# Moving work between banks and engines in a fused attention and expert kernel: two attention banks, four for the first product, a relu half on POOL

## The chip, the cores and the metric

The kernel runs on one core of a Trainium2 chip. A core has five engines that run side by side, each through its own instructions in order: PE (TensorE) multiplies matrices and writes to PSUM; DVE (VectorE) and ACT (ScalarE) work element by element on PSUM and SBUF; POOL (GpSimd) does so on SBUF alone; SP (SyncE) here only issues DMA transfers. They wait for each other by semaphores. PSUM has eight banks of 128 partitions by 2 KiB, so one bank holds 128 x 512 float32. The metric is the device time of one execution in microseconds (us). Three runs of the kernel before gave 575.06, 575.25 and 577.19 us, a median of 575.25. The profile is of one further execution, whose own time is 574.72 us.

## The reference: what is computed

Two blocks, one after the other, all in float32.

```python
def phi(x):                       # x: (4, 4, 1088, 32); S1, S2: (8, 32)
    a = np.einsum('rd,bhsd->bhsr', S1, x)
    b = np.einsum('rd,bhsd->bhsr', S2, x)
    return np.einsum('bhsi,bhsj->bhsij', a, b).reshape(*x.shape[:-1], 64)
q_p, k_p = phi(q), phi(k)
kv = np.einsum('bhsf,bhsd->bhfd', k_p, v)
z = np.sum(k_p, axis=2)
num = np.einsum('bhsf,bhfd->bhsd', q_p, kv)
den = np.einsum('bhsf,bhf->bhs', q_p, z)[..., None] + 1e-06
x = (num / den).transpose(0, 2, 1, 3).reshape(4352, 128)

p = domain_probs / (domain_probs.sum(-1, keepdims=True) + 1e-09)   # (4352, 4)
for e in range(4):                # w1: (4, 128, 1024), w2: (4, 1024, 128)
    out += p[:, e:e + 1] * (np.maximum(x @ w1[e], 0.0) @ w2[e])
```

The attention is linear: the keys of a batch are first summed into `kv`, then queries of any number can be answered. The second block is a two-layer network for each of four experts, whose outputs are added up with weights from `domain_probs`.

## The kernel before

**Chunks, steps, halves.** The 4352 tokens are columns, in chunks of 128, 448, 512, 512, 512, 512, 512, 512, 320, 256 and 128 (`CHUNKS`). A chunk has 16 steps (`kq` from 0 to 15): four experts by four pairs of blocks, and a block is 128 of an expert's 1024 hidden units. A step has two halves, j = 0 and 1, one block each. `first(i, work)` makes the first product of step i, `second(i)` the second product; the main loop calls `first(i)` and then `second(i - 2)` (`LA` is 2), so the second product runs two steps behind. The first and last chunk (`plain`) use float32 matmuls; what follows is of the nine between.

**Split numbers.** A float32 matmul is made of three matmuls on split operands. The tokens of a chunk are split by `token_parts` into xa, xb, xd, the first weights by `weight_parts` into wa, wb, wd, half of the second weights by `second_weight_parts` into `vab` (two parts in one tile) and `vd`. Each split is an ACT scaling followed by two subtractions; on DVE these are scalar_tensor_tensor operations through the helper `stt` (line 685), which scale and subtract at once; the last token part is a subtraction on POOL. Of the split weights, 24 pieces are made in all, one a step from step 5 on (`to_part`); the token pieces of a chunk are made in step 12 of the chunk before, those of the first split chunk in the last step of the plain one.

**One half of `first`** (lines 868 to 888). PE: xa by wa and xb by wb into bank `g1` (lines 871, 872), xd by wd into bank `g2` (873). ACT: `t` = scaled `g1` (875). DVE: `t` = `t` - `g2` (877). For j = 0 the relu of `t` is split again, as input of the second product: ACT makes `hb` and `ha` (894, 895), DVE corrects `hb` (898, reading `t` and `hb`), POOL subtracts `hd` = `ha` - `hb` (901). For j = 1 the relu is plain: ACT makes `hid` from `t` (887). These later operations are put into lists and emitted by `flush` one half later: `hb` and `ha` after the `t` of half j = 1; DVE's `hb` and POOL's `hd` after the subtraction of half j = 1; `hid` after the `t` of the next step's half j = 0. `work()` at the end of a half emits pieces of the attention, as many as a running account of due columns asks for.

**`second`** adds four matmuls into the two output banks: `ha`, `hb`, `hd` by their weights (950 to 952) and `hid` by plain float32 weights (954, issued as two passes). When an expert's four steps are done, that is, in every fourth call of the loop (steps 1, 5, 9 and 13 of a chunk), `gather` brings the sums out: ACT copies `ev` and `ew` (978, 979), and POOL adds them (980), multiplies by the gate (984 for the first expert, else 986) and adds to `total` (987).

**Buffers.** PSUM has three banks `h` for `g1` and `g2` in turn, two for the outputs (`o0`, `o1`), one `f` and two `den`, `num` for the attention. In SBUF the pool `mpool` has two buffers for each name unless told otherwise. `t` is told nothing, so its halves alternate: the `t` of j = 0 always has one buffer and that of j = 1 the other; `ha`, `hb`, `hd` and `hid` have three, `ev`, `ew` and `ob` one. A write waits until the readers of the buffer's former contents are through; the framework puts that wait in by itself. Each engine's order is the order in which the code emits (`manual_schedule`).

**Attention.** `front` yields the attention's pieces: `keys(b)` turns, projects (in three banks `f`, `den`, `num`), multiplies and sums the keys of a batch; `queries(b, c, n)` projects queries in `f`, works on them on DVE, and `attend` multiplies them by the summed keys in `den` and `num`, divides and stores them to memory, from where they come back as columns.

Of the kernel before, what the change touches and what calls it, by code (L numbers as in the profile page):

```python
# [8 lines left out]
F32 = mybir.dt.float32  # L9
# [15 lines left out]
def kernel(  # L25
# [51 lines left out]
    mpool = ctx.enter_context(tc.tile_pool(name="moe", bufs=2))  # L77
    ps_h = ctx.enter_context(tc.tile_pool(name="ps_h", bufs=3, space=bass.MemoryType.PSUM))
    ps_o = ctx.enter_context(tc.tile_pool(name="ps_o", bufs=1, space=bass.MemoryType.PSUM))
    ps_f = ctx.enter_context(tc.tile_pool(name="ps_f", bufs=1, space=bass.MemoryType.PSUM))  # L80
    ps_n = ctx.enter_context(tc.tile_pool(name="ps_n", bufs=1, space=bass.MemoryType.PSUM))
    dram = ctx.enter_context(tc.tile_pool(name="dram", bufs=1, space=bass.MemoryType.DRAM))
# [52 lines left out]
    def load_w2(e, j, to=None):  # L135
        w2_of[e, j] = cpool.tile([P, FB // 2, DM], F32, tag=f"w2_{e}{j}", name="w2_sb")[:, :, :] if to is None else to
        nc.sync.dma_start(w2_of[e, j], w2[e].rearrange("(f j p) d -> j p f d", j=2, p=P)[j])

# [309 lines left out]
    def keys(b):  # L448
        for r in range(3):
            key_turn(b, r)  # L450
            yield
        kf = []
        for gi, (pool, tag) in enumerate(((ps_f, "f"), (ps_n, "den"), (ps_n, "num"))):
            kf.append(psum(pool, tag))
            key_project_wide(b, gi, kf[gi])
            if gi:
                key_add(b, gi - 1, kf[gi - 1])
            yield
        for _ in value_copy(b):
# [10 lines left out]
        kv = psum(ps_f, "f")  # L470
        for p in range(2):
            key_sum(b, p, kv)
            yield
        key_blocks(b, kv)
        yield
# [48 lines left out]
    def attend_first(b, c, n, qp):  # L524

        nd = [psum(ps_n, "den"), psum(ps_n, "num")]
        for _ in range(2):
# [31 lines left out]
    def attend(b, c, n, qp):  # L559
# [3 lines left out]

        nd = [psum(ps_n, "den"), psum(ps_n, "num")]
        W = H * (D + 1)
# [74 lines left out]
    def queries(b, c, n):  # L640
        qc = early.pop((b, c), None)
        if qc is None:
            qT = query_turn(b, c, n)
            yield
            yield
            yield
            qc = psum(ps_f, "f")
            nc.tensor.matmul(qc[:, 0:n], sq[:, :], qT[:, 0:n], start=True, stop=True)
            yield
# [33 lines left out]

    def stt(out, in0, scalar, in1, op1):
        nc.vector.scalar_tensor_tensor(out=out, in0=in0, scalar=scalar, in1=in1, op0=ALU.mult, op1=op1)  # L685

    def weight_parts(e):

        HF = F // 2
        for c in (slice(0, HF), slice(HF, F)):  # L690
            nc.scalar.activation(wa[:, e, c], w1_of[e][:, c], ACTF.Copy, scale=4096.0 * NEAR)
            stt(wb[:, e, c], w1_of[e][:, c], 4096.0, wa[:, e, c].bitcast(F32), ALU.subtract)
            yield
            stt(wd[:, e, c], wa[:, e, c].bitcast(F32), R12, wb[:, e, c].bitcast(F32), ALU.subtract)
            yield
# [5 lines left out]
    def second_weight_parts(e):  # L701

        w = w2_of[e, 0]
        vab = cpool.tile([P, 2, FB // 2, DM], F32R, tag=f"w1_{e}", name="vab")
        va, vb = vab[:, 0], vab[:, 1]
        nc.scalar.activation(va, w, ACTF.Copy, scale=4096.0 * NEAR)
        stt(vb, w, 4096.0, va.bitcast(F32), ALU.subtract)
        yield
        vd = cpool.tile([P, FB // 2, DM], F32R, tag=f"w2_{e}0", name="vd")
        stt(vd[:, :, :], va.bitcast(F32), -R12, vb.bitcast(F32), ALU.add)  # L710
        w2_parts[e] = va, vb, vd
        yield
# [3 lines left out]
    def load_last():  # L716

        for e, (tag, width) in enumerate((("kn", S), ("vn", H * NT * D), ("qn", S), ("qn", S))):
            w1_of[e] = lpool.tile([P, width], F32, tag=tag, bufs=2 if tag == "qn" else 1, name="w1_last")
            nc.sync.dma_start(w1_of[e][:, 0:F], w1[e])  # L720
            if e == 0:
                w_last[0] = apool.tile([P, E, FB // 2, DM], F32, tag="kp", name="w2_last")
            load_w2(e, 0, w_last[0][:, e])
# [3 lines left out]
    def token_parts(m):  # L727
# [4 lines left out]
        nc.scalar.activation(xa[:, 0:n], x, ACTF.Copy, scale=R12 * NEAR)  # L732
        stt(xb[:, 0:n], xa[:, 0:n].bitcast(F32), -4096.0, x, ALU.add)
        nc.gpsimd.tensor_tensor(
            out=xd_[:, 0:n], in0=xa[:, 0:n].bitcast(F32), in1=xb[:, 0:n].bitcast(F32), op=ALU.subtract
        )
        xparts[m] = xa, xb, xd_

    def start():
# [16 lines left out]
        for _ in value:  # L756
            pass
        fq = [psum(ps_o, "o0"), psum(ps_o, "o1"), psum(ps_n, "num")]
        for i in range(3):
# [12 lines left out]
        key_product(b, 4, 4, 1, 1, nc.vector, kf[1])  # L772
        kv = psum(ps_f, "f")
        for t0, n0 in ((0, 4), (4, 5)):
# [58 lines left out]

    def first(i, work):

# [32 lines left out]
        for j in range(2):  # L868
# [15 lines left out]
            else:  # L884
                u = hidden()[:, 0:n]
                hid[i].append(u)
                later[ACT].append(lambda t=t, u=u: nc.scalar.activation(u, t, ACTF.Relu))  # L887
# [22 lines left out]

    def second(i):
        m, kq = steps[i]
        n, (e, f) = CHUNKS[m], divmod(kq, NP)
        hd = hid.pop(i)
        if plain(m):
# [3 lines left out]
            for j in range(2):  # L919
                for _ in range(2):  # L920
                    on_side(
                        lambda s: acc[m][half[s], 0:DM],
                        lambda s: hd[j][:, HP * s : HP * s + HP],
                        lambda s: w2_of[e, j][:, f, :],
                        start=(f == j == 0),
# [16 lines left out]
            return  # L942
        if f == 0:
# [3 lines left out]
        for j in range(2):  # L947
            if j < FK:
                (va, vb, vd), (ha, hb, hc) = w2_parts[e], hd[j]
                nc.tensor.matmul(o0, va[:, f, :], ha, start=(f == j == 0), stop=False)  # L950
                nc.tensor.matmul(o0, vb[:, f, :], hb, start=False, stop=(last and j == FK - 1))  # L951
                nc.tensor.matmul(o1, vd[:, f, :], hc, start=(f == j == 0), stop=False)  # L952
            else:
                nc.tensor.matmul(o1, w2_of[e, j][:, f, :], hd[j], start=False, stop=(last and j == 1))  # L954

# [68 lines left out]
    for i in range(len(steps) + LA):  # L1024
        if i < len(steps):
# [17 lines left out]

            first(i, work)
            if i > NQ - 12:
# [58 lines left out]
```

## Time and profile before

| | before |
|---|---|
| median of three runs | 575.25 us |
| profiled execution: its time, its span | 574.72 us, 572.9 us |
| PE busy | 501.9 us (88%) |
| DVE busy | 432.4 us (75%) |
| ACT busy | 424.5 us (74%) |
| POOL busy | 318.6 us (56%) |
| start and first plain chunk, until the first `xd,wd` matmul | 35.1 us |
| chunk of 448, to the same matmul of the next chunk | 69.3 us |
| chunks of 512 | 61.4, 62.6, 61.7, 64.3, 61.4, 61.3 us |
| chunks of 320 and of 256 | 41.9 and 34.5 us |
| last plain chunk, output | 19.4 us |

How to read the rows. The page gives for each engine the time in which it is busy, its share of the span and the instructions. The busy time of PE is modelled, since matmuls are pipelined. A row of a group of instructions has line, engine, operation, the tile written and the tiles read (buffer numbers left out), the shape, the count, then busy time, mean duration in ns, idle time of the engine just before them, and what ended that idle time. A row of the waits reads: engine and line that waited, the engine and line waited for, total us, times, longest. A row of a stretch has its bounds and length, then the busy time and count of PE, PEld (weight loads), DVE, ACT and POOL, the granted PE clock, the share of the DMA engines and GB/s. A row of the order of events has start, duration, engine, line, operation, tiles, and in brackets idle time before it.

### The profile page before, as it was taken

Reading aid. Unit: us, or ns where it says so; the run is one execution under the profiler, and the core shown is the slowest. Engines: PE = TensorE matmul, PEld = TensorE weight load, DVE = VectorE, ACT = ScalarE, POOL = GpSimd, SP = SyncE. Lnnn points to the kernel's source line nnn. Section 1 sums busy time; section 2 is a strip of 40 time slices with the busy share of each in tenths; the row PEclk is TensorE's granted clock in tenths of the full one; section 3 lists DMA queues with packets and bytes.
Section 4 is the critical chain, followed back from the end, with each engine's and each line's share of the span. In section 5 each row is a group of like instructions: output and inputs, shape, how many; then the busy total and the mean of one; then the engine's idle time right before and its main releaser. Section 6 shows DMA issues by size and latency. Waiting matters only on the chain.

```text
span 572.9 us, 9123 instructions
## 1 busy us (share of the span) xinstructions
PE 501.9 (88%) x2893; PEld 337.0 (59%) x2893; DVE 432.4 (75%) x792; ACT 424.5 (74%) x877; POOL 318.6 (56%) x298
## 2 busy tenths in 40 slices
PE   8967977989889998999798999899899888888887
PEld 5944554646555565555464556555455555666677
DVE  6969979597978777888878776778867886666643
ACT  3566766778778886878778785788778777887861
POOL 5142455456666567556565465656665666566550
PEclk9989998999999999999999998999999999999999
DMA  7661020511111212312022100021003000300700
GB/s 228 195 147 42 20 56 2 136 35 37 39 25 36 43 32 68 88 23 61 5 55 38 23 24 19 19 38 48 12 12 67 7 5 13 67 10 19 221 13 15
DMA packets 45480, 29.25 MB, mean 51 GB/s; under 512 B 26264, under 2 KB 40952, under 8 KB 45432
## 3 DMA queue, kind: packets, MB, share of 16 engines
q1 hardware_dynamic: 45416, 28.68, 19.5%
q8 instruction: 22, 0.36, 0.3%
q14 instruction: 26, 0.21, 0.1%
q10 hardware_dynamic: 16, 0.00, 0.0%
HBM read 24.42 MB, written 4.24 MB: 50 GB/s over the span
## 4 chain that ended last, share of the span: by engine, by line
PE 40%; DVE 27%; ACT 23%; issue 7%; DMA 1%; ACTq 0%; POOL 0%; SPq 0%; DVEq 0%
ACT t L875 13%; DVE t L877 9%; PE o L954 9%; DVE hb L898 9%; PE h L873 8%; PE h L871 4%; PE h L872 4%; ACT hid L887 3%; PE o L950 3%; PE o L951 3%; DVE qp L517 3%; PE o L952 3%; ACT hb L894 3%; ACT ha L895 2%; PE h L208 2%
## 5 line engine op out<-in xcount | busy, mean ns | idle before, releaser
L901 POOL TENSOR_TENSOR hd<-ha,hb 128x512 fp32r<-128x512 f32 (+3 forms) x144 | 173.2, 1203 | 206.5 <-PE h L872 74.9
L877 DVE TENSOR_TENSOR t<-t,h 128x512 f32<-128x512 f32 (+3 forms) x288 | 179.8, 625 | 116.6 <-ACT t L875 89.5
L875 ACT ACTIVATE t<-h 128x512 f32<-128x512 f32 (+3 forms) x288 | 158.9, 552 | 100.9 <-DVE hb L898 47.3
L871 PE MATMUL h<-xa,wa 128*128 128x512 f32 (+3 forms) x288 | 162.7, 565 | 12.6 <-DVE t L877 11.2
L873 PE MATMUL h<-xd,wd 128*128 128x512 f32 (+3 forms) x288 | 121.2, 421 | 48.6 <-ACT t L875 45.3
L954 PE MATMUL o<-hid,w_sb 128*128 128x512 f32 (+3 forms) x288 | 135.7, 553 | 0.0
L873 PEld LDWEIGHTS h<-xd,wd 128*128 128x128 f32 x288 | 54.4, 189 | 103.8 <-ACT t L875 96.9
L898 DVE SCALAR_TENSOR_TENSOR hb<-t,hb 128x512 fp32r<-128x512 f32 (+3 forms) x144 | 113.8, 790 | 0.3 <-ACT hb L894 0.3
L872 PE MATMUL h<-xb,wb 128*128 128x512 f32 (+3 forms) x288 | 106.8, 371 | 0.7 <-DVE xb L685 0.7
L894 ACT ACTIVATE hb<-t 128x512 fp32r<-128x512 f32 (+3 forms) x144 | 83.0, 576 | 16.0 <-DVE t L877 14.3
L871 PEld LDWEIGHTS h<-xa,wa 128*128 128x128 f32 x288 | 55.1, 191 | 58.4 <-DVE t L877 26.6
L887 ACT ACTIVATE hid<-t 128x512 f32<-128x512 f32 (+3 forms) x144 | 83.4, 579 | 0.0
L895 ACT ACTIVATE ha<-t 128x512 fp32r<-128x512 f32 (+3 forms) x144 | 82.5, 573 | 0.0
L872 PEld LDWEIGHTS h<-xb,wb 128*128 128x128 f32 x288 | 55.2, 192 | 31.1 <-issue 25.5
L954 PEld LDWEIGHTS o<-hid,w_sb 128*128 128x128 f32 x288 | 53.3, 191 | 9.2
L952 PE MATMUL o<-hd,vd 128*128 128x512 f32 (+3 forms) x144 | 54.1, 376 | 3.1 <-DVE vd L685 2.5
L950 PE MATMUL o<-ha,vab 128*128 128x512 f32 (+3 forms) x144 | 55.0, 382 | 0.0
L951 PE MATMUL o<-hb,vab 128*128 128x512 f32 (+3 forms) x144 | 53.7, 373 | 0.0
L980 POOL TENSOR_TENSOR ev<-ev,ew 128x512 f32<-128x512 f32 (+3 forms) x36 | 43.1, 1196 | 2.5 <-ACT ew L979 2.5
L987 POOL TENSOR_TENSOR total<-total,ev 128x512 f32<-128x512 f32 (+3 forms) x27 | 36.4, 1348 | 2.1
L986 POOL TENSOR_TENSOR ev<-ev,gate 128x512 f32<-128x512 f32 (+3 forms) x27 | 34.8, 1290 | 2.1
L952 PEld LDWEIGHTS o<-hd,vd 128*128 128x128 f32 x144 | 27.4, 190 | 8.4 <-POOL ev L986 2.8
(149 smaller groups left out, 495.7 us busy)
## 6 DMA issues: line engine op xcount, KB each, us to landing
gate<-gates SPq DMA_DIRECT2D x16, 256.0 KB
kn<-in_k_dram SPq DMA_DIRECT2D x4, 544.0 KB
vn<-in_v_dram SPq DMA_DIRECT2D x16, 128.0 KB
w_sb<-in_moe_w_dram SPq DMA_DIRECT2D x4, 512.0 KB
w_sb<-in_moe_w_dram SPq DMA_DIRECT2D x8, 256.0 KB
w_last<-in_moe_w_dram SPq DMA_DIRECT2D x4, 512.0 KB
gate<-gates SPq DMA_DIRECT2D x8, 224.0 KB
qn<-in_q_dram SPq DMA_DIRECT2D x2, 544.0 KB
```

The lines of the kernel that those rows point to most:

```text
L871: nc.tensor.matmul(g1[:, 0:n], wa[:, e, c], xa, start=True, stop=False)
L872: nc.tensor.matmul(g1[:, 0:n], wb[:, e, c], xb, start=False, stop=True)
L873: nc.tensor.matmul(g2[:, 0:n], wd[:, e, c], xd_, start=True, stop=True)
L875: nc.scalar.activation(t, g1[:, 0:n], ACTF.Copy, scale=1.0 + R12)
L877: nc.vector.tensor_tensor(out=t, in0=t, in1=g2[:, 0:n], op=ALU.subtract)
L887: later[ACT].append(lambda t=t, u=u: nc.scalar.activation(u, t, ACTF.Relu))
L894: nc.scalar.activation(hb, t, ACTF.Relu, scale=NEAR)
L895: nc.scalar.activation(ha, t, ACTF.Relu, scale=NEAR * R12)
L898: nc.vector.scalar_tensor_tensor(out=hb, in0=t, scalar=0.0, in1=hb.bitcast(F32), op0=ALU.max, op1=ALU.subtract)
L901: nc.gpsimd.tensor_tensor(out=hc, in0=ha.bitcast(F32), in1=hb.bitcast(F32), op=ALU.subtract)
L952: nc.tensor.matmul(o1, vd[:, f, :], hc, start=(f == j == 0), stop=False)
L954: nc.tensor.matmul(o1, w2_of[e, j][:, f, :], hd[j], start=False, stop=(last and j == 1))
```

## The change

- PSUM: the attention has two banks, `n` and `f`, in one pool instead of three; the banks `h` are four instead of three. In `keys` the three projections take `f`, `n`, `f`, and the addition that reads a bank is emitted ahead of the next projection.
- Order on PE: where the second product of step i - 2 is not the first of its expert, its half j = 0 (three matmuls) is emitted between the two halves of the first product of step i, and its half j = 1 after them.
- The pieces of weights and tokens: each DVE operation that scales and subtracts becomes an ACT scaling into a temporary tile (`tw`, in the buffers of `ob`, `ev` or `ew`) and a subtraction on POOL.
- The plain relu of `t` for j = 1 goes to POOL in odd steps, through `rectify`.
- The tiles of the second weights are two-dimensional instead of three-dimensional, with the same contents.

The diff, cut to these:

```diff
-    ps_h = ctx.enter_context(tc.tile_pool(name="ps_h", bufs=3, space=bass.MemoryType.PSUM))
+    ps_h = ctx.enter_context(tc.tile_pool(name="ps_h", bufs=4, space=bass.MemoryType.PSUM))
...
-    ps_f = ctx.enter_context(tc.tile_pool(name="ps_f", bufs=1, space=bass.MemoryType.PSUM))
-    ps_n = ctx.enter_context(tc.tile_pool(name="ps_n", bufs=1, space=bass.MemoryType.PSUM))
+    ps_a = ctx.enter_context(tc.tile_pool(name="ps_a", bufs=1, space=bass.MemoryType.PSUM))
...
-        for gi, (pool, tag) in enumerate(((ps_f, "f"), (ps_n, "den"), (ps_n, "num"))):
-            kf.append(psum(pool, tag))
-            key_project_wide(b, gi, kf[gi])
+        for gi, tag in enumerate(("f", "n", "f")):
             if gi:
                 key_add(b, gi - 1, kf[gi - 1])
+            kf.append(psum(ps_a, tag))
+            key_project_wide(b, gi, kf[gi])
             yield
...
-        nd = [psum(ps_n, "den"), psum(ps_n, "num")]
+        nd = [psum(ps_a, "n"), psum(ps_a, "f")]
...
-    def stt(out, in0, scalar, in1, op1):
-        nc.vector.scalar_tensor_tensor(out=out, in0=in0, scalar=scalar, in1=in1, op0=ALU.mult, op1=op1)
+    def scaled(tag, w, scale, dtype=F32):
+
+        t = mpool.tile([P, CW], F32, tag=tag, bufs=1, name="tw")[:, :]
+        nc.scalar.activation(t[:, 0 : w.shape[-1]].bitcast(dtype), w, ACTF.Copy, scale=scale)
+        return t
+
+    def minus(out, in0, in1):
+        nc.gpsimd.tensor_tensor(out=out, in0=in0, in1=in1, op=ALU.subtract)
...
         for c in (slice(0, HF), slice(HF, F)):
-            nc.scalar.activation(wa[:, e, c], w1_of[e][:, c], ACTF.Copy, scale=4096.0 * NEAR)
-            stt(wb[:, e, c], w1_of[e][:, c], 4096.0, wa[:, e, c].bitcast(F32), ALU.subtract)
-            yield
-            stt(wd[:, e, c], wa[:, e, c].bitcast(F32), R12, wb[:, e, c].bitcast(F32), ALU.subtract)
+            w, a, b, d = (x[:, c] for x in (w1_of[e], wa[:, e], wb[:, e], wd[:, e]))
+            nc.scalar.activation(a, w, ACTF.Copy, scale=4096.0 * NEAR)
+            minus(b, scaled("ob", w, 4096.0), a.bitcast(F32))
+            yield
+            minus(d, scaled("ev", w, NEAR, F32R), b.bitcast(F32))
             yield
...
-        stt(xb[:, 0:n], xa[:, 0:n].bitcast(F32), -4096.0, x, ALU.add)
-        nc.gpsimd.tensor_tensor(
-            out=xd_[:, 0:n], in0=xa[:, 0:n].bitcast(F32), in1=xb[:, 0:n].bitcast(F32), op=ALU.subtract
-        )
+        minus(xb[:, 0:n], x, scaled("ew", x, NEAR, F32R)[:, 0:n])
+        minus(xd_[:, 0:n], xa[:, 0:n].bitcast(F32), xb[:, 0:n].bitcast(F32))
...
-                later[ACT].append(lambda t=t, u=u: nc.scalar.activation(u, t, ACTF.Relu))
+                later[ACT].append(lambda t=t, u=u: rectify(u, t, kq % 2))
             work()
+            if between and j == 0:
+                between(0)
+
+    def rectify(u, t, on_pool):
+        if on_pool:
+            nc.gpsimd.tensor_scalar(out=u, in0=t, scalar1=0.0, scalar2=None, op0=ALU.max)
+        else:
+            nc.scalar.activation(u, t, ACTF.Relu)
...
-            first(i, work)
+            parted = i >= LA and not plain(steps[i - LA][0]) and not plain(m) and steps[i - LA][1] % NP
+            first(i, work, (lambda j: second(i - LA, j)) if parted else None)
...
-            second(i - LA)
+            second(i - LA, 1 if i < len(steps) and parted else None)
```

More of the change, by code (lines that the diff above doesn't have):

```diff
@@ L135, in load_w2 @@
     def load_w2(e, j, to=None):
-        w2_of[e, j] = cpool.tile([P, FB // 2, DM], F32, tag=f"w2_{e}{j}", name="w2_sb")[:, :, :] if to is None else to
-        nc.sync.dma_start(w2_of[e, j], w2[e].rearrange("(f j p) d -> j p f d", j=2, p=P)[j])
+        w2_of[e, j] = cpool.tile([P, FB // 2 * DM], F32, tag=f"w2_{e}{j}", name="w2_sb")[:, :] if to is None else to
+        nc.sync.dma_start(
+            w2_of[e, j].rearrange("p (f d) -> p f d", d=DM), w2[e].rearrange("(f j p) d -> j p f d", j=2, p=P)[j]
+        )
     load_rows(k, 0, "kn")
@@ L469, in keys @@
         yield
-        kv = psum(ps_f, "f")
+        kv = psum(ps_a, "n")
         for p in range(2):
@@ L524, in attend_first @@
     def attend_first(b, c, n, qp):
-        nd = [psum(ps_n, "den"), psum(ps_n, "num")]
+        nd = [psum(ps_a, "n"), psum(ps_h, "h")]
         for _ in range(2):
@@ L559, in attend @@
     def attend(b, c, n, qp):
-        nd = [psum(ps_n, "den"), psum(ps_n, "num")]
+        nd = [psum(ps_a, "n"), psum(ps_a, "f")]
         W = H * (D + 1)
@@ L646, in queries @@
             yield
-            qc = psum(ps_f, "f")
+            qc = psum(ps_a, "f")
             nc.tensor.matmul(qc[:, 0:n], sq[:, :], qT[:, 0:n], start=True, stop=True)
@@ L703, in second_weight_parts @@
         w = w2_of[e, 0]
[L704 to L707, printed above, removed]
+        vab = cpool.tile([P, 2, FB // 2 * DM], F32R, tag=f"w1_{e}", name="vab")
+        a, b = vab[:, 0], vab[:, 1]
+        nc.scalar.activation(a, w, ACTF.Copy, scale=4096.0 * NEAR)
+        minus(b, scaled("ob", w, 4096.0), a.bitcast(F32))
         yield
-        vd = cpool.tile([P, FB // 2, DM], F32R, tag=f"w2_{e}0", name="vd")
-        stt(vd[:, :, :], va.bitcast(F32), -R12, vb.bitcast(F32), ALU.add)
-        w2_parts[e] = va, vb, vd
+        u = scaled("ev", w, NEAR, F32R)
+        d = cpool.tile([P, FB // 2 * DM], F32R, tag=f"w2_{e}0", name="vd")[:, :]
+        minus(d, b.bitcast(F32), u)
+        w2_parts[e] = a, b, d
         yield
@@ L721, in load_last @@
             if e == 0:
-                w_last[0] = apool.tile([P, E, FB // 2, DM], F32, tag="kp", name="w2_last")
+                w_last[0] = apool.tile([P, E, FB // 2 * DM], F32, tag="kp", name="w2_last")
             load_w2(e, 0, w_last[0][:, e])
@@ L757, in start @@
             pass
-        fq = [psum(ps_o, "o0"), psum(ps_o, "o1"), psum(ps_n, "num")]
+        fq = [psum(ps_o, "o0"), psum(ps_o, "o1"), psum(ps_a, "n")]
         for i in range(3):
@@ L772, in start @@
         key_product(b, 4, 4, 1, 1, nc.vector, kf[1])
-        kv = psum(ps_f, "f")
+        kv = psum(ps_a, "f")
         for t0, n0 in ((0, 4), (4, 5)):
@@ L832, in half_columns, with first @@
             )
-    def first(i, work):
+    def first(i, work, between=None):
         m, kq = steps[i]
@@ L909, in flush, with second @@
                 later[w].pop(0)()
-    def second(i):
+    def second(i, j=None):
         m, kq = steps[i]
         n, (e, f) = CHUNKS[m], divmod(kq, NP)
-        hd = hid.pop(i)
+        hd = hid[i] if j == 0 else hid.pop(i)
         if plain(m):
@@ L923, in second @@
                         lambda s: hd[j][:, HP * s : HP * s + HP],
-                        lambda s: w2_of[e, j][:, f, :],
+                        lambda s: w2_of[e, j][:, DM * f : DM * (f + 1)],
                         start=(f == j == 0),
@@ L942, in second @@
             return
-        if f == 0:
+        if f == 0 and j in (0, None):
             acc[m, e] = psum(ps_o, "o0"), psum(ps_o, "o1")
@@ L946, in second @@
         last = f == NP - 1
-        for j in range(2):
+        w = slice(DM * f, DM * (f + 1))
+        for j in range(2) if j is None else (j,):
             if j < FK:
                 (va, vb, vd), (ha, hb, hc) = w2_parts[e], hd[j]
-                nc.tensor.matmul(o0, va[:, f, :], ha, start=(f == j == 0), stop=False)
-                nc.tensor.matmul(o0, vb[:, f, :], hb, start=False, stop=(last and j == FK - 1))
-                nc.tensor.matmul(o1, vd[:, f, :], hc, start=(f == j == 0), stop=False)
+                nc.tensor.matmul(o0, va[:, w], ha, start=(f == j == 0), stop=False)
+                nc.tensor.matmul(o0, vb[:, w], hb, start=False, stop=(last and j == FK - 1))
+                nc.tensor.matmul(o1, vd[:, w], hc, start=(f == j == 0), stop=False)
             else:
-                nc.tensor.matmul(o1, w2_of[e, j][:, f, :], hd[j], start=False, stop=(last and j == 1))
+                nc.tensor.matmul(o1, w2_of[e, j][:, w], hd[j], start=False, stop=(last and j == 1))
     def turn_back(m, src):
@@ L1061 @@
         if i == LA:
-            made_hp[3] = psum(ps_n, "num")
+            made_hp[3] = psum(ps_h, "h")
             for c in (0, HP):
```

## The prediction

> **What bounds the kernel now.** I read the page's sums first, then the stretches of the trace chunk by chunk, then the waits, then the order of events in one undisturbed stretch. On the page:
>
> ```profile
> span 572.9 us, 9123 instructions
> PE 501.9 (88%) x2893; PEld 337.0 (59%) x2893; DVE 432.4 (75%) x792; ACT 424.5 (74%) x877; POOL 318.6 (56%) x298
> ```
>
> No engine is full. The stretches (PE, PEld, DVE, ACT, POOL busy) are cut at the first `xd,wd` matmul of a chunk; here are one chunk of 512 columns, the one of 320 and the one of 256:
>
> ```profile
> 354.40:415.80 61.40, 54.99 (x242) 34.23 (x240) 49.02 (x83) 48.35 (x89) 36.40 (x28) 1.00 0.13 28
> 477.10:519.00 41.90, 35.13 (x179) 27.45 (x178) 27.18 (x55) 34.24 (x89) 25.49 (x28) 1.00 0.13 30
> 519.00:553.50 34.50, 28.41 (x176) 23.83 (x174) 20.88 (x49) 28.57 (x89) 20.18 (x27) 1.00 0.33 101
> ```
>
> The six chunks of 512 take 61.4, 62.6, 61.7, 64.3, 61.4 and 61.3 us, 372.7 together, so four steps take 15.5 us and one step 3.9. The 448 chunk takes 69.3 (35.1 to 104.4), the start 35.1, the last plain chunk 19.4. What is waited for (us in total, times, longest):
>
> ```profile
> PEld h L873 <- ACT t L875: 96.9, 133, 2.0
> DVE t L877 <- ACT t L875: 89.5, 152, 2.4
> ACT t L875 <- DVE hb L898: 47.3, 52, 2.1
> PE h L873 <- ACT t L875: 45.3, 83, 1.6
> ```
>
> Lines 1 and 4 are the three banks: the third matmul of a half takes the bank that the ACT evacuation of the half before has to free. Line 3 is another ring: `t` has two buffers, so the `t` of a half j=0 waits until the DVE operation of line 898, one step earlier, has read its buffer. Keep that ring in mind. The order of events, undisturbed:
>
> ```profile
> 417.98 0.60 ACT L875 ACTIVATE t<-h 128x512 f32<-128x512 f32 x1
> 418.47 0.62 ACT L894 ACTIVATE hb<-t 128x512 fp32r<-128x512 f32 x1
> 418.61 0.69 DVE L877 TENSOR_TENSOR t<-t,h 128x512 f32<-128x512 f32 x1 [0.46 <-ACT t L875]
> 418.99 0.62 ACT L895 ACTIVATE ha<-t 128x512 fp32r<-128x512 f32 x1
> 419.21 0.68 DVE L898 SCALAR_TENSOR_TENSOR hb<-t,hb 128x512 fp32r<-128x512 f32 x1
> 420.07 1.28 POOL L901 TENSOR_TENSOR hd<-ha,hb 128x512 fp32r<-128x512 f32 x1 [1.90 <-PE h L872]
> 420.57 0.62 ACT L887 ACTIVATE hid<-t 128x512 f32<-128x512 f32 x1
> ```
>
> The durations come from here; the steps between engines too: 0.04 us from ACT to DVE and back, 0.18 from DVE (419.89) to POOL (420.07). POOL to PE is 0.06 elsewhere (`xd` ends 35.02, its matmul starts 35.08).
>
> **The change, part by part.**
>
> *Four banks, alternating products.* They remove the bank wait: in the chain a bare step is 3.25 us (0.50 third matmul + 1.55 second product + 0.47 + 0.61 ACT and 0.12 between), while the matmuls alone take 9 x 0.23 + 0.86 = 2.93. The gain is at most 0.32 a bare step and more in disturbed ones, if nothing else is late. What is late next decides, so I count no gain here; it is in the walk below and in rival 1.
>
> *Attention in two banks.* Its pieces run one after another, and the addition is now emitted ahead of the projection that takes its bank. Cover: the pieces between. Without it, three batches wait about 1 us each; bounds 0 to 3, taken 0.
>
> *Half of the plain relu on POOL.* This is the step that counts. Odd steps give ACT 0.62 us less. But `t` keeps two buffers: the `t` of half j=1 in step i+1 (ACT) overwrites what POOL's relu of step i reads, and so now waits for it. On POOL that relu is emitted behind `hd` of step i, and in every second odd step also behind the three gather operations (ev, product, total). Queued behind the waiting `t` on ACT are `hb`, `ha` and the next `t`; waiting for those are DVE, the bank of the next first product, and through `hb` the very `hd` that the next POOL relu is queued behind. That closes a loop over two steps, counted from the start of such a `t` (512 columns, i odd):
>
> - ACT t 0 to 0.60; DVE subtraction 0.64 to 1.33, hb 1.33 to 2.02 (ACT's hb and ha end at 1.84);
> - ACT t j=0 of step i+2 needs that hb: 2.06 to 2.66, ACT relu to 3.28, t j=1 to 3.88;
> - DVE subtraction 3.92 to 4.61, hb to 5.30; POOL hd 5.48 to 6.76;
> - POOL relu 6.83 to 6.83 + r; 0.06 later the next `t` that waits for POOL starts.
>
> So a pair of steps takes 6.89 + r, and every second pair has the gather in it: 3 x (1.285 + 0.07) = 4.06 us, by the medians of lines 980, 986 and 984 (987 has 1.425, partly beside DVE). Its ACT copies (1.2) hide under hd. PE hides as well: its next matmuls are released at 0.64 and 2.70 and need 2.9 a step.
>
> The relu on POOL is not in the trace. Nearest rows:
>
> ```profile
> L734 POOL TENSOR_TENSOR xd<-xa,xb 128x512 fp32r<-128x512 f32 x6 | 7.7, 1282 | 4.4 <-DVE xb L685 4.4
> L782 POOL COPY sq<-s_T 32x32 f32<-32x32 f32 x4 | 0.8, 203 | 0.2
> L174 POOL MEMSET sr<- 128x768 f32 x1 | 0.7, 742 | 0.0
> L263 POOL COPY sr<-sp 32x192 f32<-32x192 f32 x2 | 0.7, 338 | 0.1
> L282 POOL TENSOR_SCALAR dsum<-dsum 128x34 f32<-128x34 f32 x1 | 0.2, 224 | 0.1
> L173 POOL MEMSET sk<- 128x128 f32 x1 | 0.2, 205 | 0.3 <-POOLq L1088 0.3
> ```
>
> The two copies give 0.84 ns an element above 0.18: 0.61 at 512. The same operation at 34 elements gives 1.41 ns: 0.90. I take the middle, r = 0.75 (448: 0.68, 320: 0.54, 256: 0.46). Bounds: the memsets, 0.53, and two inputs, 1.28. The Trainium skill's "GPSIMD Engine Reference", Elementwise, has 769 ns for a tight loop over 512 elements; as an estimate that would make r = 0.77 and the sum 1 us longer.
>
> Four steps of 512: 2 x 7.64 + 4.06 = 19.34, a chunk 77.4. On top, per chunk: 1.0 for the second ACT operation of the token pieces; 0.6 for half of ACT's attention copies (2.7 a batch, half a batch a chunk); 2.0 for DVE attention pieces of 0.7 us where the loop leaves only 0.5 to 0.7 (eight pairs by 0.25): 81.0, against 62.1. Six chunks: 485.7 - 372.7 = **+113**.
> The 320 chunk by its rows (t 0.44, relu 0.465, subtraction 0.49, hd 0.88): pair 5.06 + 0.54, gather 2.83: 8 x 5.60 + 4 x 2.83 + 2 = 58.1: **+16.2**. The 256 chunk: pair 4.88, gather 2.4: 8 x 4.88 + 9.6 + 0.5 = 49.1: **+14.6**.
>
> *Pieces of weights and tokens.* 32 subtractions leave DVE (0.99 mean for wb, 1.475 for xb) for POOL (1.28), with 32 more ACT operations (0.62). In the 448 chunk 13 of the 24 weight pieces fall into the loop: the six in odd steps sit on POOL between hd and relu (6 x 1.35 = 8.1); in even steps ACT gets 0.4 beyond its slack (six: 2.4). Chunk: 8 x 6.88 + 3 x 3.6 + 8.1 + 2.4 + 2 = 78.3 against 69.3: **+9**. In the first 35 us, 11 pieces of 1.35 go through POOL from about 20 us, with 3.2 us of ring copies, then two token operations of 1.2: ready at about 40.4 instead of 35.1: **+5** (bounds 0, if POOL starts with the first weights, and 8).
>
> Sum: 113 + 16.2 + 14.6 + 9 + 5 = 158 on the profiled execution's 574.7: **732 us**. That execution lies 0.5 below the median of 575.25, which changes nothing at this size. The last plain chunk keeps its 19.4.
>
> Ends: with r = 0.53, no extras and no loss at the start: 6 x 75.6 - 372.7 = 81, 12 + 12 for the short chunks, 3 for 448: 683. With r = 1.28, 72 waits of 0.5 more: 768; with all the extras doubled (six by 3.6) 790.
>
> A rule that speaks against the change: line 898 takes 0.684 median, but 0.866 mean at 512, up to 1.79, where POOL works beside it. The Trainium skill's "SBUF — State Buffer", Who interferes with whom, says that a DVE instruction with two SBUF inputs and a GpSimd one that reads SBUF exclude each other for whole instructions. By it, busier POOL would add 0.58 to each colliding hb; if half of 144 collide, 42 us. By the walk the two run in turn (POOL idle from 0 to 2.0 and 4.6 to 5.5), so I add nothing.
>
> **Rivals.**
> 1. *Faster: the wait on POOL does not decide.* Then four steps take what the fullest engine needs: PE 11.7 + 1.4 of attention = 13.1, ACT 12.2 + 0.8, DVE about 12, POOL 11.3. Halfway between 13.1 and 15.5, at 14.2, 24 groups of four win 31, the short chunks 4, and 5 are lost at the start: 545. For it: the bank waits (142 us on PE) really go. Against: it needs two pairs and the gather to stay under 15.5 together; even with the gather outside, two pairs are 15.3. It decides only if POOL's relu starts before hd and the gather.
> 2. *Same: the gather hides, the relu wait stays.* 15.3 for 15.5, extras against bank waits: 575.
> 3. *POOL's relu costs as much as two inputs:* 768.
> 4. *The clock falls.* PE would stand about 4 us in every gather pair; at half clock for a while, 1 us more in each of 35 groups: 767. The page has the clock under full in 3 of 40 slices, without such gaps.
>
> **How the numbers follow.** The forecast has 0.65, rival 3 0.12, rival 4 0.10, a milder loop (under 690) 0.06, rival 1 0.04, rival 2 0.03. Rivals 3 and 4 end near 770, the bounds at 683 and 790: the range is 680 to 790, outside of which lie rivals 1 and 2 and parts of the others, about 0.15. Slower has 0.93, same 0.03, faster 0.04; half a per cent, 2.9 us, is about what a measurement of this kernel can tell.
>
> **What would show it.** In the profile after: ACT's `t` waiting for POOL's `hid` as the largest wait, over 150 us in some 72 waits, long (over 4 us) in every second; four steps of 512 at 19 to 20 us; POOL's relu at 0.6 to 0.9; the old waits of the third matmul for ACT `t` mostly gone, replaced by PE waiting for `t` behind POOL; ACT and PE shares down to about 60 to 70%. A `t` that hardly waits for POOL, or relus on POOL ahead of the gather, would make all this wrong. Weight pieces: the 448 chunk near 78 us, its start near 40.

## The result and the profile after

The changed kernel takes 762.61 us (median of four runs, 762.04 to 763.53), the kernel before 576.13 (four runs, 575.06 to 577.19). The ratio is 1.324, with a 95% interval of 1.320 to 1.327: 186 us slower. The prediction said 732 us in a range of 680 to 790. The direction and the place were right; the sum is 30 us short.

The profiled execution took 762.66 us, with these rows on its page: the sums by engine, the granted clock in 40 slices, the shares of the chain that ended last, POOL's relu and DVE's `hb` (line 913 is line 898 of before).

```profile
span 760.9 us, 9052 instructions
PE 582.0 (76%) x2893; PEld 375.0 (49%) x2893; DVE 384.7 (51%) x759; ACT 404.7 (53%) x838; POOL 445.4 (59%) x403
...
PEclk9888887999998888999988989988988999889899
...
POOL 33%; PE 29%; ACT 13%; DVE 12%; issue 9%; DMA 2%; SPq 1%; POOLq 0%; ACTq 0%; DVEq 0%
...
L901 POOL TENSOR_SCALAR hid<-t 128x512 f32<-128x512 f32 (+3 forms) x72 | 99.7, 1385 | 0.0
...
L913 DVE SCALAR_TENSOR_TENSOR hb<-t,hb 128x512 fp32r<-128x512 f32 (+3 forms) x144 | 92.7, 644 | 0.0
```

No engine is full, as before, but POOL, which was nowhere on the chain of before (0%), now makes the largest share of it with only 59% of its time busy. The chain of before, for comparison:

```profile
PE 40%; DVE 27%; ACT 23%; issue 7%; DMA 1%; ACTq 0%; POOL 0%; SPq 0%; DVEq 0%
```

A share of busy time does not show a bound of this kind; the waits of the changed kernel do:

```profile
DVE t L884 <- ACT t L882: 332.3, 223, 6.4
ACT t L882 <- POOL hid L901: 249.3, 65, 6.5
PEld h L878 <- ACT t L882: 186.9, 137, 5.4
...
PE h L878 <- ACT t L882: 124.2, 56, 4.9
PEld h L880 <- DVE t L884: 51.5, 118, 2.4
...
PE f L393 <- DVE fs L403: 12.7, 2, 6.7
...
PEld o L969 <- POOL vd L692: 8.9, 1, 8.9
PE o L969 <- POOL vd L692: 8.6, 1, 8.6
```

The second row is the new one: ACT stands 249 us before 65 of its `t`, until POOL's relu has read the buffer. DVE and PE then stand behind ACT (first, third and fourth row). Line 878 is the first matmul of a half; the old waits of the third matmul (now 880) for ACT's `t` have shrunk from 142 us to 7.6. So the four banks did what they were for, but only in part: the third matmul now waits 65 us for DVE's `t` (51.5 of them in the fifth row), against 0.7 before, and PE stands longest one matmul further on, at the first of the next half.

The stretches, cut as those of before: the chunk of 448, one of 512, those of 320 and 256 (length; then busy time of PE, PEld, DVE, ACT, POOL; granted clock; DMA share and GB/s):

```profile
39.10:128.70 89.60, 63.27 (x268) 41.09 (x269) 46.58 (x82) 49.61 (x105) 56.91 (x47) 0.83 0.21 47
128.70:211.20 82.50, 65.84 (x274) 37.54 (x272) 44.80 (x83) 43.07 (x80) 48.32 (x36) 0.92 0.10 26
634.70:691.80 57.10, 44.09 (x178) 32.04 (x176) 23.56 (x53) 30.40 (x80) 34.54 (x37) 0.88 0.10 22
691.80:740.20 48.40, 38.19 (x175) 28.67 (x174) 19.16 (x49) 26.24 (x80) 26.50 (x35) 0.89 0.24 72
```

| stretch, us | before | predicted | after |
|---|---|---|---|
| start | 35.1 | 40.4 | 39.1 |
| chunk of 448 | 69.3 | 78.3 | 89.6 |
| six of 512 | 372.7 | 485.7 | 506.0 |
| chunk of 320 | 41.9 | 58.1 | 57.1 |
| chunk of 256 | 34.5 | 49.1 | 48.4 |
| last plain chunk | 19.4 | 19.4 | 20.7 |

The loop itself, in the timeline of an undisturbed pair of steps (165.13 to 173.17) and a pair with the gather in it (173.17 to 185.15). Some rows are left out; a bracket gives the idle time before and what ended it:

```profile
165.13 0.60 ACT L882 ACTIVATE t<-h 128x512 f32<-128x512 f32 x1 [5.21 <-POOL hid L901]
165.62 0.62 ACT L909 ACTIVATE hb<-t 128x512 fp32r<-128x512 f32 x1
...
167.16 0.60 ACT L882 ACTIVATE t<-h 128x512 f32<-128x512 f32 x1 [0.40 <-DVE hb L913]
...
167.66 0.62 ACT L903 ACTIVATE hid<-t 128x512 f32<-128x512 f32 x1
...
168.31 0.60 ACT L882 ACTIVATE t<-h 128x512 f32<-128x512 f32 x1
...
169.55 0.68 DVE L913 SCALAR_TENSOR_TENSOR hb<-t,hb 128x512 fp32r<-128x512 f32 x1
...
170.40 1.28 POOL L916 TENSOR_TENSOR hd<-ha,hb 128x512 fp32r<-128x512 f32 x1 [1.90 <-DVE rc L590]
171.65 1.49 POOL L901 TENSOR_SCALAR hid<-t 128x512 f32<-128x512 f32 x1
173.17 0.60 ACT L882 ACTIVATE t<-h 128x512 f32<-128x512 f32 x1 [2.23 <-POOL hid L901]
...
178.44 1.29 POOL L916 TENSOR_TENSOR hd<-ha,hb 128x512 fp32r<-128x512 f32 x1 [1.89 <-PE h L879]
179.69 1.28 POOL L997 TENSOR_TENSOR ev<-ev,ew 128x512 f32<-128x512 f32 x1
181.04 1.28 POOL L1003 TENSOR_TENSOR ev<-ev,gate 128x512 f32<-128x512 f32 x1
182.40 1.26 POOL L1004 TENSOR_TENSOR total<-total,ev 128x512 f32<-128x512 f32 x1
183.63 1.48 POOL L901 TENSOR_SCALAR hid<-t 128x512 f32<-128x512 f32 x1
185.15 0.60 ACT L882 ACTIVATE t<-h 128x512 f32<-128x512 f32 x1 [5.70 <-POOL hid L901]
```

The order is the one walked through in the prediction: `hd`, three gather operations, relu, and 0.03 to 0.04 us later the `t` that waited. What differs most is the relu: 1.48 to 1.49 us, longer than the 1.28 of a subtraction of two tiles.

### The profile page after: what moved, and what is told of

It is laid out like the page before. It is cut to its first block, busy times and chain, and to the rows that moved or that the text cites. A ratio compares the mean times of both kernels' runs of the same rounds, so it can differ in the third digit from the quotient of the medians.

```text
span 760.9 us, 9052 instructions
## 1 busy us (share of the span) xinstructions
PE 582.0 (76%) x2893; PEld 375.0 (49%) x2893; DVE 384.7 (51%) x759; ACT 404.7 (53%) x838; POOL 445.4 (59%) x403
## 3 DMA queue, kind: packets, MB, share of 16 engines
q1 hardware_dynamic: 45416, 28.68, 14.8%
## 4 chain that ended last, share of the span: by engine, by line
POOL 33%; PE 29%; ACT 13%; DVE 12%; issue 9%; DMA 2%; SPq 1%; POOLq 0%; ACTq 0%; DVEq 0%
POOL hid L901 11%; ACT t L882 8%; PE o L971 6%; POOL hd L916 6%; POOL ev L997 5%; PE h L878 5%; DVE t L884 5%; PE h L880 5%; DVE hb L913 5%; POOL ev L1003 4%; POOL total L1004 4%; PE h L879 4%; PE n L209 2%; ACT hid L903 1%; POOL total L1001 1%
## 5 line engine op out<-in xcount | busy, mean ns | idle before, releaser
L878 PE MATMUL h<-xa,wa 128*128 128x512 f32 (+3 forms) x288 | 178.2, 619 | 128.4 <-ACT t L882 124.2
L878 PEld LDWEIGHTS h<-xa,wa 128*128 128x128 f32 x288 | 62.6, 217 | 211.1 <-ACT t L882 186.9
L971 PE MATMUL o<-hid,w_sb 128*128 128x512 f32 (+3 forms) x288 | 159.1, 639 | 0.0
L880 PE MATMUL h<-xd,wd 128*128 128x512 f32 (+3 forms) x288 | 128.6, 446 | 17.0 <-DVE t L884 13.8
L879 PE MATMUL h<-xb,wb 128*128 128x512 f32 (+3 forms) x288 | 116.0, 403 | 1.7 <-POOL xb L692 1.7
L901 POOL TENSOR_SCALAR hid<-t 128x512 f32<-128x512 f32 (+3 forms) x72 | 99.7, 1385 | 0.0
L913 DVE SCALAR_TENSOR_TENSOR hb<-t,hb 128x512 fp32r<-128x512 f32 (+3 forms) x144 | 92.7, 644 | 0.0
L880 PEld LDWEIGHTS h<-xd,wd 128*128 128x128 f32 x288 | 60.5, 210 | 64.3 <-DVE t L884 51.5
L879 PEld LDWEIGHTS h<-xb,wb 128*128 128x128 f32 x288 | 62.6, 217 | 31.2 <-issue 25.5
L903 ACT ACTIVATE hid<-t 128x512 f32<-128x512 f32 (+3 forms) x72 | 41.4, 576 | 0.0
L967 PEld LDWEIGHTS o<-ha,vab 128*128 128x128 f32 x144 | 30.5, 212 | 11.8 <-ACT ev L995 7.6
```

The lines of the kernel that those rows point to most:

```text
L878: nc.tensor.matmul(g1[:, 0:n], wa[:, e, c], xa, start=True, stop=False)
L879: nc.tensor.matmul(g1[:, 0:n], wb[:, e, c], xb, start=False, stop=True)
L880: nc.tensor.matmul(g2[:, 0:n], wd[:, e, c], xd_, start=True, stop=True)
L901: nc.gpsimd.tensor_scalar(out=u, in0=t, scalar1=0.0, scalar2=None, op0=ALU.max)
L913: nc.vector.scalar_tensor_tensor(out=hb, in0=t, scalar=0.0, in1=hb.bitcast(F32), op0=ALU.max, op1=ALU.subtract)
L967: nc.tensor.matmul(o0, va[:, w], ha, start=(f == j == 0), stop=False)
```

## Experiments

Theory: the `t` that waits for POOL's relu makes the whole loss. Rivals: the pieces of weights and tokens on POOL, the alternating order on PE, the falling clock, or POOL's load as such. The times in this section are medians of four runs or more, unless said otherwise; the kernel before, on the same chips, had 576.4, 576.4 and 576.0 us in the three groups.

**1. The relu back on ACT, all else as changed.**

```diff
-                later[ACT].append(lambda t=t, u=u: rectify(u, t, kq % 2))
+                later[ACT].append(lambda t=t, u=u: rectify(u, t, False))
```

> The changed kernel with the plain relu on ACT in all steps again; all else of the change stays. Theory (the loop): nothing waits for a relu on POOL; four steps take what the fullest engine needs, 13.5 to 15 us, 6 chunks of 512 in 330 to 360 us, the start still about 39 us; in all 540 to 575 us. Rival (the pieces of weights and tokens on POOL, or the banks, make the loss): over 650 us.

Measured: 573.09 us, ratio 0.994 (0.992 to 0.996). One word in the diff is worth 189.5 us, more than the loss; the rest of the change is 3 us better than nothing.

**2. The relu on POOL, and nothing else of the change.** The kernel before with the function `rectify` and the call above.

> The kernel before, with one part of the change alone: the plain relu of odd steps on POOL. Theory (the loop): the same two-step loop arises without any other part: relus 8.0 and 12.0 us apart, four steps 20 to 21 us, six chunks of 512 in about 490 to 510 us, the start as before; in all 700 to 750 us. Rival (the loss needs the order of both products or the pieces on POOL): 575 to 620 us.

Measured: 767.2 us, ratio 1.333 (1.328 to 1.337). That is above the expectation, and 5 us above the whole change. Its waits:

```profile
ACT t L875 <- POOL hid L892: 211.3, 60, 6.6
...
PE h L873 <- ACT t L875: 135.4, 92, 4.6
```

The relu alone makes the loss, and with three banks PE waits for the same `t` at the third matmul (line 873). Pieces, order and banks are out as causes.

**3. The relu on POOL, but its `t` out of the ring.** In odd steps the `t` of j = 1 is made in a `hid` tile (three buffers), and POOL's relu works in place, so that no later `t` has to wait for POOL.

```diff
-            t = mpool.tile([P, CW], F32, tag="t", name="t")[:, 0:n]
+            t = (hidden() if j and kq % 2 else mpool.tile([P, CW], F32, tag="t", name="t"))[:, 0:n]
...
-                u = hidden()[:, 0:n]
+                u = t if kq % 2 else hidden()[:, 0:n]
```

> The changed kernel, with one thing different: in odd steps the t of half j=1 is written into the hid tile (three buffers) and POOL's relu works in place there, so that no later t waits for it. POOL does the same operations in the same order, and as much work. Theory (the loop through the two buffers of t): ACT's wait for POOL's hid, 249 us in the changed kernel, is gone; the time between the ends of two POOL relus falls from 8.0 and 12.0 us in turn to about 7.5 on average. What is left is that the second product of an odd step needs the relu that stands behind the gather: about 3 us of PE per four steps, so four steps take 15 to 16.5 us and the kernel 560 to 620 us. Rival (POOL is simply too slow for what it was given, or the weight and token pieces cost it): POOL's order and load are the same, so the time stays above 700 us.

Measured: 629.72 us, ratio 1.092 (1.086 to 1.098), 10 us over the expectation's upper end. Without the loop through the ring the kernel is 133 us faster. The other 57 (629.7 - 573.1) stay as long as the relu is on POOL:

```profile
ACT t L882 <- PE h L879: 121.7, 60, 6.1
PEld o L971 <- POOL hid L901: 92.2, 37, 4.9
PE o L971 <- POOL hid L901: 79.9, 36, 4.5
```

PE's second product now stands 80 us, 36 times, until POOL, behind `hd` and the gather, has made `hid`. So the wait on the buffer was the larger part, and even without it POOL's queue would have been late for the next reader. This edit also leaves the ring with three tiles instead of four in every two steps, and so eases its older wait too (in every step, and without POOL, that is worth 24.6 us, see experiment 8): 133 may hold some of that, and 57 may be too small by as much. POOL's load as such, the same in this run, is in any case not what makes most of the loss.

**4. What POOL takes for each form.** Six operations of 128 x 512 in the kernel before, put into the last plain chunk, where POOL is idle; one run of 577.69 us.

```diff
...
+                nc.gpsimd.memset(pin[:, :], 0.5)
+                nc.gpsimd.tensor_copy(pout[:, :], pin[:, :])
+                nc.gpsimd.tensor_scalar(out=pout[:, :], in0=pin[:, :], scalar1=0.0, scalar2=None, op0=ALU.max)
+                nc.gpsimd.tensor_scalar(out=pout[:, :], in0=pin[:, :], scalar1=0.0, scalar2=1.0, op0=ALU.max, op1=ALU.mult)
+                nc.gpsimd.tensor_scalar(out=pout[:, :], in0=pin[:, :], scalar1=0.0, scalar2=1.0, op0=ALU.add, op1=ALU.mult)
+                nc.gpsimd.tensor_tensor(out=pout[:, :], in0=pin[:, :], in1=pin[:, :], op=ALU.subtract)
```

> The kernel before with six extra POOL operations on 128x512 tiles in the last plain chunk, where POOL and DVE's SBUF side are idle: memset, copy, the relu form (maximum with 0, one operation), maximum and multiplication, addition and multiplication, and a subtraction of two tiles. They change no result. Theory A (the relu of the changed kernel took 1.485 us because of the operation itself): the maximum takes 1.4 to 1.5 us here too, while memset and copy take 0.53 and 0.61. Theory B (its neighbours slowed it): the maximum takes 0.6 to 0.9 us. The form with addition and multiplication tells whether the row at 34 elements (0.224 us) could have shown it. The kernel's time stays at 576 us.

Measured, in the same order (min/median/max ns, first and last start):

```profile
L1048 POOL MEMSET pin<- x1: 529/529/529, 562.3 to 562.3; 128x512 f32 x1
L1049 POOL COPY pout<-pin x1: 611/611/611, 562.9 to 562.9; 128x512 f32<-128x512 f32 x1
L1050 POOL TENSOR_SCALAR pout<-pin x1: 1493/1493/1493, 563.6 to 563.6; 128x512 f32<-128x512 f32 x1
L1051 POOL TENSOR_SCALAR pout<-pin x1: 1926/1926/1926, 565.2 to 565.2; 128x512 f32<-128x512 f32 x1
L1052 POOL TENSOR_SCALAR pout<-pin x1: 619/619/619, 567.2 to 567.2; 128x512 f32<-128x512 f32 x1
L1053 POOL TENSOR_TENSOR pout<-pin x1: 1041/1041/1041, 567.9 to 567.9; 128x512 f32<-128x512 f32 x1
```

The estimates from copies and memsets (0.61 and 0.53) held. But one and the same instruction, on one and the same shape, takes 0.62 us with addition and multiplication and 1.49 with a maximum: it is the maximum that is dear. Other engines were at work beside this test, DVE beside the maximum and not beside the addition, but that does not explain it: of the 48 relus of 512 columns in the changed kernel, 25 ran with no DVE operation beside them, and each took 1.48 to 1.49 us. One is that of 183.63 above, during which ACT, DVE and PE all stood.

**5. The changed kernel with the cheap form in the relu's place.** POOL adds 0 and multiplies by 1, so the wait stays and only its price changes. (The plain half of odd steps is thus left without its relu.)

```diff
-            nc.gpsimd.tensor_scalar(out=u, in0=t, scalar1=0.0, scalar2=None, op0=ALU.max)
+            nc.gpsimd.tensor_scalar(out=u, in0=t, scalar1=0.0, scalar2=1.0, op0=ALU.add, op1=ALU.mult)
```

> The changed kernel with POOL's operation on t replaced by t + 0 times 1, the form that took 0.62 us alone where the maximum took 1.49. In odd steps the plain half is thus left without its relu, so the output is not the reference's; everything else is as in the changed kernel. Theory (r stands in the loop once for each pair of steps): 72 times 0.87 less, scaled by the chunks' widths 57 us, that is 700 to 710 us, and the relus' ends 7.1 and 11.2 us apart instead of 8.0 and 12.0. Rival (the loop's length is not set by r): within 15 us of 762.

Measured: 709.95 us, ratio 1.232 (1.229 to 1.236), at the upper edge of the expectation. The row of POOL's operation, from the page:

```profile
L901 POOL TENSOR_SCALAR hid<-t 128x512 f32<-128x512 f32 (+3 forms) x72 | 44.1, 612 | 0.0
```

With r smaller by 0.87 us at 512, a pair without the gather shrinks from 8.04 to 7.17 us, by the same 0.87: the relu lies on the path with its whole length. The kernel gets 52.7 us faster, and is still 134 us slower than before: the dear form is the smaller part of the loss, the loop the larger.

**6. Banks and order without the pieces.** Experiment 1 with the subtractions of weights and tokens back on DVE, as before.

```diff
-            minus(b, scaled("ob", w, 4096.0), a.bitcast(F32))
+            stt(b, w, 4096.0, a.bitcast(F32), ALU.subtract)
...
-            minus(d, scaled("ev", w, NEAR, F32R), b.bitcast(F32))
+            stt(d, a.bitcast(F32), R12, b.bitcast(F32), ALU.subtract)
...
-        minus(xb[:, 0:n], x, scaled("ew", x, NEAR, F32R)[:, 0:n])
+        stt(xb[:, 0:n], xa[:, 0:n].bitcast(F32), -4096.0, x, ALU.add)
```

> The changed kernel with the plain relu on ACT and the pieces of weights and tokens on DVE as before: what is left of the change are the banks and the alternating order. Theory: the waits of the third matmul for ACT's t (142 us before) are mostly gone, DVE with its 12.2 us per four steps and ACT with 13.0 become the limits, and the kernel takes 540 to 570 us; against the run with the pieces on ACT and POOL it shows what these are worth, by the estimate 5 us lost at the start and 1 to 1.5 us won per chunk boundary. Rival (the shorter distance between first and second product stalls PE on POOL's hd): 575 us or more.

Measured: 565.98 us, ratio 0.983 (0.980 to 0.986). The pieces on ACT and POOL cost 7.1 us (573.09 - 565.98), of which the start alone is 4.8 (39.5 against 34.7 us).

**7. Banks without the alternating order.**

```diff
-            parted = i >= LA and not plain(steps[i - LA][0]) and not plain(m) and steps[i - LA][1] % NP
-            first(i, work, (lambda j: second(i - LA, j)) if parted else None)
+            parted = False
+            first(i, work)
```

> The kernel before with the banks of the change alone (four for the first product, two for the attention); order, relu and pieces as before. Theory (the bank wait was worth something and the order little): 564 to 570 us, like the run with banks and order. Rival (only the alternating order lets PE use the fourth bank): 573 to 578 us.

Measured: 561.52 us, ratio 0.975 (0.973 to 0.977), a little better than expected. The alternating order costs 4.5 us. So the parts, each added to those before it: banks -14.8, order +4.5, pieces +7.1, relu +189.5.

**8. The `t` ring emptied, with the relu on ACT.** The wait of `t` for the step before was in the kernel before too (47 us, for DVE's `hb`). Experiment 6, with the `t` of every half j = 1 in a `hid` tile and ACT's relu in place:

```diff
-            t = mpool.tile([P, CW], F32, tag="t", name="t")[:, 0:n]
+            t = (hidden() if j else mpool.tile([P, CW], F32, tag="t", name="t"))[:, 0:n]
...
-                u = hidden()[:, 0:n]
+                u = t
```

> Banks and order of the change, pieces on DVE, relu on ACT in all steps, and the t of every half j=1 written into the hid tile and made positive in place, so that the two buffers of t serve the halves j=0 alone. ACT's wait for DVE's hb (56 us in the run with banks and order) goes, since that buffer now has a whole step more. Theory (this wait is on the path in part): 552 to 562 us. Rival (it is slack that another wait takes over): 564 to 568 us.

Measured: 541.37 us, ratio 0.938 (0.935 to 0.942), better than expected by 11 to 21 us.

**9. The same, with the token pieces on ACT and POOL** (one line, `stt` for `xb` replaced by `minus` and `scaled` as in the change).

> The run before this one with the token pieces as the change has them (a second ACT scaling and a subtraction on POOL instead of 1.475 us on DVE, nine times). Theory (DVE is what ends these steps): 5 to 12 us faster than the run before. Rival (ACT's 0.62 and POOL's 1.28 cost as much): within 3 us of it, or slower.

Measured: 543.76 us, ratio 0.944 (0.942 to 0.945). It is not 5 to 12 us faster; the 2.4 us by which it is slower lie within the spread of the runs of experiment 8 (537.65 to 542.60). So DVE, though busier there than ACT (81 against 77% of the span), was not the limit that the expectation took it for.

**10. Banks and in-place tile, without the alternating order**: experiment 7 with the edit of experiment 8.

> The kernel before with the banks of the change and the t of half j=1 in the hid tile, relu on ACT in place; no alternating order, no pieces moved. Theory (the alternating order only shortens the distance between the products, and cost 4.5 us without the in-place tile): 532 to 540 us, faster than the 541 with that order. Rival (with t out of the way PE needs the alternating order): 542 us or more.

Measured: **529.49 us** (529.46 to 529.54), ratio 0.920 (0.917 to 0.922): the best version here, 46.5 us under the kernel before. Its page:

```profile
span 527.4 us, 9023 instructions
PE 481.5 (91%) x2893; PEld 344.5 (65%) x2893; DVE 436.6 (83%) x792; ACT 409.9 (78%) x877; POOL 324.0 (61%) x298
```

The order now costs 11.9 us (541.37 - 529.49). Most of it is seen where PE takes POOL's `hd` (line 971 in both). First experiment 8, with the alternating order, then this one:

```profile
PEld o L971 <- POOL hd L918: 25.2, 24, 3.0
...
PE o L971 <- POOL hd L918: 15.8, 16, 2.6
```

```profile
PEld o L971 <- POOL hd L918: 10.2, 9, 2.0
PE o L971 <- POOL hd L918: 5.9, 8, 1.4
```

The half j = 0 of the second product, moved ahead of half j = 1 of the first, asks for `hd` earlier, and PE, which works in order, stands 9.9 us longer for it (15.8 against 5.9), of 10.3 us by which it stands longer in all. The two executions that were profiled are 8.2 us apart (537.65 and 529.46).

**11. The in-place tile alone, on the kernel before** (three banks, its own order; the edit of experiment 8).

> The kernel before with the in-place tile alone, three banks as before. Theory (the waits for a bank and for t stand in one chain, so that the gain of one needs the other): 565 to 576 us, less than the 15 us that banks won and the 25 that the tile won on top. Rival (the two add up): 548 to 556 us.

Measured: 552.47 us, ratio 0.961 (0.957 to 0.966). The rival was right: 23.5 us, not 0 to 11. Banks alone win 14.8, the tile alone 23.5, both together 46.5: more than the 38.3 of their sum. The waits fit that: with the banks alone, ACT still stands 52.0 us for DVE's `hb` before it writes `t`; with the tile alone, PE still stands 77.9 us for ACT's `t` at the third matmul (63.5 + 14.4, weight loads and matmuls). Each leaves the other's wait in place.

## Why the prediction was right, and what was wrong in it

**The place was right.** It named the `t` of j = 1 waiting for POOL's relu as the largest new wait, above 150 us in some 72 waits, over 4 us in every second. Found: 249 us in 65, up to 6.5. Experiments 1 and 2 show from both sides that this part alone makes the loss, and experiment 3 that the ring makes about 133 of the 190.

**The step that failed: r, the relu on POOL**, taken as 0.75 us with bounds of 0.53 and 1.28. Measured at 512 columns: 1.48 (median; the mean is 1.54), so outside the bounds; at 448, 320 and 256: 1.40, 1.00 and 0.84 (means). By the prediction's own formula that adds 48 x 0.73 + 8 x 0.72 + 8 x 0.46 + 8 x 0.38 = 48 us. The rows it was worked out from were copies, memsets and a 34-column operation that, as its line of code says, adds and multiplies; experiment 4 shows that those are right for what they are and say nothing of a maximum. The upper bound took it that an operation with one input can't cost more than one with two. The Trainium skill's "GPSIMD Engine Reference", Engine selection, likewise calls operations with one input roughly line-rate on GpSimd; for the maximum the runs show 1.49 us against 1.28 for two tiles, and the measurement decides.

**The hops were too long.** With r = 1.49 the walk gives 6.89 + 1.49 = 8.38 us for a pair; the timeline shows 8.04. The walk let each operation begin after the last one's recorded end, but ACT's relu begins at 167.66, 0.50 after a `t` that is recorded with 0.60, and POOL's relu at 171.65, before `hd`'s 170.40 + 1.28. The prediction's own rows show such a start: `hb` at 418.47, 0.49 after a `t` of 0.60. Experiment 5 gives the same difference with another r: 7.17 against 6.89 + 0.62 = 7.51. Over 72 pairs that is about -24 us, an estimate from 512 columns. The two errors had opposite signs: r alone would have made the sum 780, and the hops, by luck, took half of that back.

**The chunk of 448: 89.6 for 78.3.** The relu makes 5.8 of it (8 x 0.72), and the shorter hops take 2.7 off. About another 6 are a wait that the prediction did not have: `vd` of the third expert is made in the very step that needs it. In the waits of before PE stood 2.5 us for it, made by DVE. Now it is on POOL, behind the relu and `hd`:

```profile
91.45 1.32 POOL L901 TENSOR_SCALAR hid<-t 128x448 f32<-128x448 f32 x1
94.71 1.13 POOL L916 TENSOR_TENSOR hd<-ha,hb 128x448 fp32r<-128x448 f32 x1 [1.94 <-DVE hb L913]
95.80 1.26 POOL L692 TENSOR_TENSOR vd<-vab,tw 128x512 fp32r<-128x512 f32 x1
```

PE starts the matmul at 97.12, after 8.6 us of standing. The pair of steps that begins at 92.81 takes 15.4 us, until 108.24; the other pairs without the gather in this chunk take 8.7 to 9.3. The six pieces were costed as time in the loop; who waits for them was not asked.

**Attention in two banks: 0, bounds 0 to 3.** Wrong in the bound: PE stood 12.7 us in two of three batches (`PE f L393`), because the addition that frees bank `f` needs an ACT copy, and ACT's queue stands behind the waiting `t`. In experiment 1, with the same banks and without the loop, these two waits are 0.5 and 1.3 us. The cover named, "the pieces between", was gone once the loop was there. The two chunks with these batches are longer than the median of the other four (82.7) by 6.7 and 3.7 us, against 1.2 and 2.9 before, so about 6 us of it are in the time. The chunks without keys have extras of some 2.5 us instead of 3.6, and that pays it back.

**Sum.** Of the 30 us, the six chunks of 512 make 20.3, the chunk of 448 11.3, all others together -1.7.

**Rivals.** Rival 3, a relu as costly as two inputs, at 768, is what came true in kind; it had a chance of 0.12. The relu is dearer still (1.48 against 1.28), and that the number is nearly met is owed in part to the shorter hops. Rival 4, the falling clock, came true in its condition and not in its price. The granted clock falls from 0.988 to 0.883 in the mean, but here are the pair from above and two more pairs without the gather, each from one `t` that waited for POOL to the next (the column before the last two is the clock):

```profile
165.13:173.17 8.04, 7.14 (x22) 3.69 (x22) 5.02 (x11) 4.98 (x10) 4.01 (x3) 1.00 0.10 24
378.91:386.95 8.04, 7.39 (x49) 4.97 (x49) 4.90 (x11) 4.98 (x10) 4.01 (x3) 0.79 0.11 19
507.19:515.23 8.04, 7.39 (x17) 4.88 (x17) 4.73 (x9) 4.98 (x9) 4.01 (x3) 0.58 0.23 29
```

At 0.58 and 0.79 of full clock the pair takes the same 8.04 us: PE has the slack to be slow. Of the 24 pairs of 512 columns without the gather, 11 take 8.03 to 8.06 us, at clocks from 0.58 to 1.00. In the others more comes together (attention, longer relus), and what the clock adds there is not shown. Rivals 1 and 2 needed the wait not to decide; experiment 1, without it, gives 573, near rival 2's 575 and not rival 1's 545. The rule on the shared port of SBUF was rightly left out of the sum: `hb` on DVE takes 0.644 us in the mean, against 0.790 in this row of before:

```profile
L898 DVE SCALAR_TENSOR_TENSOR hb<-t,hb 128x512 fp32r<-128x512 f32 (+3 forms) x144 | 113.8, 790 | 0.3 <-ACT hb L894 0.3
```

Of its 96 operations of 512 columns, 28 overlapped an operation of POOL in the kernel before and took 1.31 us in the mean, the others 0.68; in the changed kernel 4 did, since DVE and POOL mostly work in turn in the loop. In the fast version of experiment 10 it is 47 of 96, and the mean of all `hb` is 0.850.

**Other signs.** The start came at 39.1 (40.4 predicted), the old bank wait went as predicted. Four steps of 512 take 20.0 us in the timeline (8.04 + 11.98) and 20.6 in the chunk of 82.50, just over the 19 to 20 named. ACT and PE were to fall to 60 to 70%; they have 53 and 76. No sum stood behind these shares: ACT's busy time hardly changed (424.5 to 404.7 us), and 404.7 in 732 would already be 55%; PE's busy time grew from 501.9 to 582.0, with longer matmuls at the lower clock.

## What to carry to other kernels

Before a reader of a tile is moved to another engine, ask who writes that tile's buffer next and what stands ahead of the reader in its new queue: here the loop that this question finds made about 133 of the 190 us, and the relu's place behind the rest of POOL's queue most of the others. The ring with two buffers gave 23.5 us when relieved of one half in the kernel before, 46.5 with the banks. Price an operation by a row with the same arithmetic, not only the same engine and shape; where there is none, the upper bound has to leave room for more than the nearest rows. Add up a chain from starts, not from recorded ends, and let covers be checked against the kernel as it will be, not as it was.

## What the runs showed of the hardware that was not expected

- On POOL, the tensor-scalar instruction on 128 x 512 float32 took 0.619 us with addition and multiplication, 1.493 with a maximum, 1.926 with a maximum and a multiplication; a copy took 0.611. A subtraction of a tile from itself took 1.041, of two tiles 1.28. (Those in experiment 4 were run once each; the maximum ran 25 times with no DVE operation beside it in the changed kernel, at 1.48 to 1.49.)
- ACT's operations of 512 columns, recorded with 0.60 to 0.62 us, began 0.49 to 0.53 us after one another where nothing held them (165.13, 165.62, 166.14).
- PE's granted clock was under 0.9 in 20 of 40 slices of the changed kernel; undisturbed pairs of steps took 8.04 us at 0.58 as at 1.00, since PE was not late there.
- A DVE operation that reads two tiles of SBUF took 0.68 us where no POOL operation overlapped it and 1.31 in the mean where one did (28 of the 96 `hb` of 512 columns in the kernel before).
